# Rebuilding the front of an attention-then-MoE kernel: load order, masking and upsampling by matmul, and a first stage begun operand by operand

## The chip, the cores and the metric

The kernel runs on one core of a Trainium2 chip. The metric is device time in microseconds (us); a profile's span is a little shorter.

In the profile, PE is TensorE (matmul), PEld its weight loads, ACT ScalarE, DVE VectorE, POOL GpSimd, and SP SyncE, which issues DMAs. A trailing q (SPq, ACTq) is an engine's sequencer. "Half clock" means that the TensorE clock granted in the records was 0.50 instead of 1.00.

## The reference, cut to what matters

```python
# 8 batches, 8 heads, 576 tokens, head size 64
q_d, k_d, v_d = (mean over each 4 tokens of q, k, v)
out_up    = repeat(softmax(q_d k_d^T / 8) v_d, 4)                      # 144 tokens, upsampled
out_local = softmax(where(|i - j| < 4, q k^T / 8, -1e9)) v
x = (out_up + out_local) as [4608, 512]
h = x @ w_in                             # 512 -> 2048, "first stage"
out = (h * sigmoid(1.702 h)) @ w_out     # 2048 -> 512, "second stage"
```

## The kernel before

The MoE works on nine groups of 512 tokens. During group g, TensorE also does the attention of batch g+1, slipped in at fixed steps. So only the attention of batch 0 stands exposed, in the prologue. The first stage has 16 blocks of four matmuls (one per operand `xT[0..3]`, that is, per head pair), each block followed by a silu on ScalarE. The second stage has four output tiles of 16 matmuls.

The matmuls of this kernel write their results to PSUM. A tile of 512 FP32 columns is called one bank here, and the program declares eight of them: three two-bank tiles rotate in the attention, two one-bank accumulators rotate in the MoE:

```python
psA = tile_pool(name="psA", bufs=3, PSUM)       # [128, 2, 512] FP32: two banks each
psM = tile_pool(name="psM", bufs=2, PSUM)       # [128, 512] FP32: one bank each
...
def mm1(g, steps):
    for ffc in range(16):
        for f in steps.get(ffc, ()): f()        # attention of the next batch
        hps = psM.tile([128, TG], FP32, name="hps", tag="psM")
        for dmc in range(4):
            nc.tensor.matmul(hps, lhsT=w_in_bf[:, dmc, ...], rhs=xT[dmc][:, ...], ...)
        nc.scalar.activation(out=gT[:, ffc, :], in_=hps, func=AF.Silu, scale=1.702)
```

The prologue and the loads around it:

```python
load_v(0)                        # 10 DMAs issued by SyncE
load_qk(0, 0); load_qk(0, 1)     # issued by GpSimd (they cast to bf16)
...  # pooling on GpSimd, exp, band mask on VectorE, av, four normalisations, transposes
load_w_in(0, 512)                # issued on GpSimd after the pooling of batch 0
load_w_in(512, 512); load_w_in(1024, 1024)
for qd in range(2): load_qk(1, qd)
load_w_out(0)
...
for hp in range(4):              # transposes; upsampled part copied, then added ("merge")
    x[hp] = transp(y[hp]); merge(0, hp, x[hp], copy_od(x[hp]), ...)
load_v(1, gate=gate)             # SyncE
for c in range(1, 4): load_w_out(c)
...
osb = moe_sb.tile([128, n], FP32, name="osb", tag=f"osb{n}", bufs=3)   # scaled output, then a store on SyncE
```

The softmax here doesn't subtract the row's maximum and nothing guards it: scores larger than these inputs give would overflow.

## Time and profile before

| | |
|---|---|
| time | 337.35 us (337.05 to 337.67) |
| PE busy | 94% of the span |
| chain of waits | PE 84%, SPq 5%, DMA 4% |
| last operand of batch 0 ready | 31.47 us |
| TensorE idle in group 0 | 50.0 to 56.3 us |
| distance from one group's first silu to the next, from group 1 to group 7 | 33.5 to 34.4 us |

A row of the last kind says most about a steady state: it is read from the timeline as the start of the first silu of each group.

In the steady state (timeline of the kernel before, columns: start us, duration us, engine, line, operation, output<-inputs, shapes, count, idle time before and what ended it), a block of four matmuls passes every 0.86 us:

```profile
215.64 0.60 ACT L523 ACTIVATE gT<-hps 128x512 bf16<-128x512 f32 x1 [0.27 <-PE hps L517]
215.66 0.38 PE L517 MATMUL hps<-xT_83,w_in_bf 128*128 128x512 bf16 x1
215.88 0.38 PE L517 MATMUL hps<-xT_84,w_in_bf 128*128 128x512 bf16 x1
216.09 0.38 PE L517 MATMUL hps<-xT_85,w_in_bf 128*128 128x512 bf16 x1
216.31 0.38 PE L517 MATMUL hps<-xT_82,w_in_bf 128*128 128x512 bf16 x1
216.51 0.60 ACT L523 ACTIVATE gT<-hps 128x512 bf16<-128x512 f32 x1 [0.27 <-PE hps L517]
```

The matmuls start 0.216 us apart.

TensorE's longest waits (waits view; columns: total us, times, longest us):

```profile
PE vdp L272 <- POOL vb_87 L251: 6.3, 1, 6.3
PE sl_188 L299 <- DVE qT_179 L220: 3.3, 1, 3.3
```

The first is the hole in group 0: v of batch 1 is late. The windows view shows what it costs beyond the idle time (columns: window, its length, busy us of PE, PEld, DVE, ACT, POOL with counts, granted PE clock, DMA share, GB/s):

```profile
50.00:52.00 2.00, 0.01 (x1) 0.04 (x1) 0.00 (x0) 0.08 (x1) 0.00 (x0) 1.00 1.02 168
54.00:56.00 2.00, 0.00 (x0) 0.00 (x0) 0.00 (x0) 0.00 (x0) 2.00 (x1) 0.50 0.02 4
60.00:62.00 2.00, 2.00 (x6) 0.72 (x5) 0.56 (x2) 1.98 (x3) 0.00 (x0) 0.50 0.00 0
```

TensorE idles at 50 to 56, and afterwards works at half clock until about 62. The idle time began at 50.0, and the mean clock of 0.60 in the window from 52 to 54 puts the fall at about 52.4, so 2.4 us later. The clock came back at about 62.6 (mean 0.84 from 62 to 64), 6.3 us after the work had resumed.

### The profile page before, as it was taken

The page shows a single profiled execution, that of the slowest core. Times are in us where ns is not written, and L with a number is a line of the kernel's source. Part 1 is how long each engine was busy: PE and PEld are TensorE (multiplying, and loading weights), DVE is VectorE, ACT ScalarE, POOL GpSimd, SP SyncE. Part 2 cuts the span into 40 slices and gives each one's busy share as a digit, 9 for nine tenths or more (in the row PEclk, how much of TensorE's full clock was granted, in tenths as well). Part 3 has the DMA queues.
Part 4 walks back from the last instruction along what each step waited for, and adds up shares of the span by engine and source line. Part 5 has one row for each costly group of instructions (what it writes and reads, how often), then busy time and mean ns, then how long its engine had stood idle before and what let it go on. Part 6 is the DMA issues. An engine that isn't in the chain of part 4 may idle for free.

```text
span 336.2 us, 11213 instructions
## 1 busy us (share of the span) xinstructions
PE 315.9 (94%) x5013; PEld 157.4 (47%) x5013; DVE 135.3 (40%) x217; ACT 184.2 (55%) x315; POOL 138.6 (41%) x164
## 2 busy tenths in 40 slices
PE   6777993999999999999999999999999999999995
PEld 2343442454545455545554545455545554444444
DVE  5766710384067506750675066506750570000000
ACT  2346760546664667466746673668366737424611
POOL 6966802027940892089208920793079000000000
PEclk9699996799999999999999999999999999999999
DMA  8899992199991897199519951898180010011012
GB/s 148 150 159 211 196 200 42 67 181 198 262 190 68 164 204 139 64 181 204 120 67 188 204 114 66 161 208 135 66 163 13 33 67 31 2 63 62 0 55 71
DMA packets 63552, 41.36 MB, mean 123 GB/s; under 512 B 44048, under 2 KB 54416, under 8 KB 63504
## 3 DMA queue, kind: packets, MB, share of 16 engines
q1 hardware_dynamic: 55056, 26.95, 37.5%
q0 software_dynamic: 8304, 13.63, 23.0%
q8 instruction: 39, 0.64, 0.8%
q14 instruction: 9, 0.07, 0.1%
q10 hardware_dynamic: 144, 0.07, 0.1%
HBM read 44.83 MB, written 9.44 MB: 161 GB/s over the span
## 4 chain that ended last, share of the span: by engine, by line
PE 84%; SPq 5%; DMA 4%; POOL 2%; DVE 2%; issue 1%; ACT 1%; POOLq 0%; ACTq 0%
PE ops L558 36%; PE hps L517 33%; SPq L174 5%; DMA qb_128<-in_q_dram 2%; PE sd L315 2%; PE av L354 2%; PE xt L403 2%; PE av L376 2%; DMA vf<-in_v_dram 1%; PE ops L572 1%; PE vdp L272 1%; POOL vb_87 L251 1%; PE warm L465 1%; DVE y L389 1%; PE xt L413 0%
## 5 line engine op out<-in xcount | busy, mean ns | idle before, releaser
L558 PE MATMUL ops<-w_out_bf,gT 128*128 128x512 bf16 x560 | 129.8, 383 | 0.0
L523 ACT ACTIVATE gT<-hps 128x512 bf16<-128x512 f32 x144 | 86.0, 597 | 49.0 <-PE hps L517 49.0
L517 PEld LDWEIGHTS <-w_in_bf 128*128 128x128 bf16 x576 | 55.8, 98 | 68.4 <-issue 2.0
L558 PEld LDWEIGHTS <-gT 128*128 128x128 bf16 x560 | 52.2, 98 | 60.8 <-issue 2.1
L517 PE MATMUL hps<-xT_85,w_in_bf 128*128 128x512 bf16 x144 | 54.6, 379 | 0.8 <-DVE vf L590 0.8
L517 PE MATMUL hps<-xT_82,w_in_bf 128*128 128x512 bf16 x144 | 54.6, 379 | 0.0
L517 PE MATMUL hps<-xT_84,w_in_bf 128*128 128x512 bf16 x144 | 54.6, 379 | 0.0
L517 PE MATMUL hps<-xT_83,w_in_bf 128*128 128x512 bf16 x144 | 54.6, 379 | 0.0
L543 ACT ACTIVATE osb<-ops 128x512 f32<-128x512 f32 (+2 forms) x37 | 22.0, 595 | 40.4 <-PE ops L558 27.2
L340 DVE TENSOR_TENSOR es_90<-es_90,mask 128x600 bf16<-128x600 bf16 x8 | 7.6, 950 | 84.8 <-ACT es_90 L326 84.8
L425 ACT COPY od<-xt 128x384 f32<-128x384 f32 x64 | 21.1, 412 | 36.3 <-PE xt L413 30.8
L389 DVE TENSOR_TENSOR y<-av,rc 128x896 bf16<-128x896 f32 x32 | 34.9, 1092 | 1.1
L545 DVE TENSOR_SCALAR osb<-ops 128x128 f32<-128x128 f32 x1 | 0.3, 291 | 55.3 <-ACT osb L543 55.3
L387 DVE RECIPROCAL rc<-av 128x14 f32<-128x14 f32 x32 | 7.7, 240 | 19.6 <-PE av L376 19.6
L465 PE MATMUL warm<-wz 128*128 128x512 bf16 x41 | 14.1, 476 | 1.2 <-DVE wz L100 1.2
L251 POOL CAST vb_87<-vf 128x2560 bf16<-128x2560 f32 x4 | 9.4, 2344 | 13.1 <-DMA vf<-in_v_dram 13.1
L403 PEld LDWEIGHTS <-y 60*64 60x64 bf16 x640 | 7.4, 107 | 9.2 <-issue 4.3
L403 PE MATMUL xt<-ident,y 60*64 60x57 bf16 (+1 forms) x640 | 9.5, 194 | 1.3 <-issue 0.8
L340 DVE TENSOR_TENSOR es_92<-es_92,mask 128x600 bf16<-128x600 bf16 x8 | 4.2, 529 | 13.8 <-ACT es_92 L326 13.8
L482 ACT ACT_TABLE_LOAD x7 | 9.0, 1283 | 0.1
L478 ACT ACT_TABLE_LOAD x7 | 9.0, 1283 | 0.1
L446 DVE TENSOR_TENSOR xT_84<-xt,od 128x570 bf16<-128x570 f32 x8 | 6.0, 754 | 7.1 <-ACT od L425 7.1
(335 smaller groups left out, 382.5 us busy)
## 6 DMA issues: line engine op xcount, KB each, us to landing
vf<-in_v_dram SPq DMA_DIRECT2D x80, 128.0 KB, 6.6
out_dram<-osb SPq DMA_DIRECT2D x35, 256.0 KB, 2.1
v_96<-in_v_dram SPq DMA_DIRECT2D x36, 192.0 KB, 5.4
w_out_bf<-in_moe_w_out_dram POOLq DMA_DIRECT2D x4, 512.0 KB, 18.0
w_in_bf<-in_moe_w_in_dram POOLq DMA_DIRECT2D x2, 512.0 KB, 6.6
w_in_bf<-in_moe_w_in_dram POOLq DMA_DIRECT2D x1, 1024.0 KB, 11.6
kb_116<-in_k_dram POOLq DMA_DIRECT2D x1, 288.0 KB, 5.3
qb_118<-in_q_dram POOLq DMA_DIRECT2D x1, 288.0 KB, 6.7
```

Source lines behind the costliest of these rows:

```text
L174: nc.sync.dma_start(out=t[64 * par : 64 * par + 64, i], in_=bass.AP(tensor=v.tensor, offset=v[b, 0].offset + (114 * i + KSTART[par]) * D, ...
L251: cp(out=vbs[b % 2][:, i, h, 0:D], in_=vf[b][:, i, h])
L340: nc.vector.tensor_tensor(out=ev, in0=ev, in1=mask, op=ALU.mult)
L389: nc.vector.tensor_tensor(out=y, in0=ov[:, :, :, 0:D], in1=rc.to_broadcast([128, 2, 7, D]), op=ALU.mult,)
L403: nc.tensor.matmul(x[64 * j : 64 * j + 64, par, 57 * i + c0 : 57 * i + c1], lhsT=y[64 * pos : 64 * pos + 60, par, i, :], rhs=ident[64 * po ...
L425: nc.scalar.copy(out=od[:, 4 * t0 : 4 * (t0 + n)].rearrange("p (t f) -> p t f", f=4), in_=x[:, xx, 288 : 288 + n, None].to_broadcast([128, ...
L465: nc.tensor.matmul(t, lhsT=wz[:, 0:128], rhs=wz, start=True, stop=True)
L478: nc.scalar.preload_act_table_set("exp_and_others")
L517: nc.tensor.matmul(hps, lhsT=w_in_bf[:, dmc, ffc * 128 : (ffc + 1) * 128], rhs=xT[dmc][:, tok0 : tok0 + TG], start=(dmc == 0), stop=(dmc = ...
L523: nc.scalar.activation(out=gT[:, ffc, :], in_=hps, func=AF.Silu, scale=GELU_SCALE)
L543: eng.activation(out=osb, in_=ap, func=AF.Copy, scale=1.0 / GELU_SCALE)
L558: nc.tensor.matmul(ops[t], lhsT=gT[:, ffc, t * 128 : (t + 1) * 128], rhs=w_out_bf[:, ffc, :], start=(ffc == 0), stop=(ffc == n_ffc - 1),)
```

## The change

Its intent is to shorten the two stretches at the front that TensorE does not bound. The prologue is rebuilt: v of batch 0 waits for the first k and goes out on two queues (SyncE and ScalarE), w_in is gated behind a piece of v, the band mask of batch 0 is added in PSUM by matmul, and the upsampling becomes part of the transposing matmuls. Four PSUM tiles of two banks are held by name (`PA`), so that the four head pairs have one each. The first six blocks of group 0 are begun as each operand arrives. v of batch 1 now comes ahead of w_out 2 and 3, and the second stage of group 0 is reordered to need them late. The core of the diff, with cuts:

```diff
-    psA = ... tile_pool(name="psA", bufs=3, PSUM)
-    psM = ... tile_pool(name="psM", bufs=2, PSUM)
+    psum = ... tile_pool(name="psum", bufs=1, PSUM)
+    PA = [psum.tile([128, 2, 512], FP32, name=f"pa{i}") for i in range(4)]
+    PM = [PA[3][:, u, :] for u in range(2)]
+    def pm_tile():
+        turn["m"] += 1
+        return PM[turn["m"] % 2]
 ...
-            hps = psM.tile([128, TG], FP32, name="hps", tag="psM")
+            hps = acc[ffc % 8] if g == 0 else pm_tile()
 ...
-                ops[t] = psM.tile([128, d_model], FP32, name="ops", tag="psM")
+                ops[t] = PA[0][:, t - 2, :] if g == 0 and t > 1 else pm_tile()
 ...
+    load_v(0, gate=after_k, queues=(nc.sync, nc.scalar))
 ...
+    sp = scores(0, 0, barred=True)              # mask added in PSUM
+    nc.gpsimd.tensor_copy(out=w_in_bf[0:1, 0, 0:1], in_=vf[0][0:1, 1, 0, 0:1])
     load_w_in(0, 512)
 ...
+    warm(7); sd = scores_d(0, 0); ...; warm(4); ...; warm(5)    # dummy matmuls
+    prep_vd_pe(0, PA[3])
 ...
+    def spark(n):                               # short dummy matmuls
+        for _ in range(n):
+            nc.tensor.matmul(PA[3][:, 1, 456:512], lhsT=wz[:, 0:128], rhs=wz[:, 0:56], ...)
+    acc = [PA[n][:, u, :] for n in range(4) for u in range(2)]
+    spark(8); turned(0); spark(4); turned(1)    # turned: transp_sum and copy of one head pair
+    part((0, 1), 0); turned(2); ...; turned(3); part((0, 1, 2, 3), 2); ...
+    for ffc in range(6): silu(gT0, ffc, acc[ffc])
 ...
     def loads_2():
-        load_qk(2, 0, gate=gate); load_qk(2, 1)
-        load_v(2)
+        load_v(2, gate=gate)
         load_v4(2)
 ...
+            load_v(1, gate=after(w_out_bf[0:1, 0, 0:1], nc.vector))
+            nc.gpsimd.tensor_copy(out=w_out_bf[0:1, 8, 0:1], in_=vf[1][0:1, 2, 0, 0:1])
+            load_w_out(2); load_w_out(3)
```

More of the change, by code (lines that the diff above doesn't have):

```diff
@@ L51 @@
     moe_sb = ctx.enter_context(tc.tile_pool(name="moe_sb", bufs=1))
-    psA = ctx.enter_context(
-        tc.tile_pool(name="psA", bufs=3, space=bass.MemoryType.PSUM)
-    )
-    psM = ctx.enter_context(
-        tc.tile_pool(name="psM", bufs=2, space=bass.MemoryType.PSUM)
+    psum = ctx.enter_context(
+        tc.tile_pool(name="psum", bufs=1, space=bass.MemoryType.PSUM)
     )
@@ L69, with ps_tile @@
     kdT = [persist.tile([128, 160, 2], BF16, name=f"kdT{i}") for i in range(NQ)]
+    PA = [psum.tile([128, 2, 512], FP32, name=f"pa{i}") for i in range(4)]
+    PM = [PA[3][:, u, :] for u in range(2)]
+    turn = {"a": 0, "m": 0}
+    def ps_tile(n=None):
+        if n is None:
+            n = turn["a"] % 3
+            turn["a"] += 1
+        return PA[n]
+    def pm_tile():
+        turn["m"] += 1
+        return PM[turn["m"] % 2]
+    UP = 5 + 240
     wz = consts.tile([128, 512], BF16, name="wz")
+    off = consts.tile([128, 60], BF16, name="off")
     psel = consts.tile([128, 7, 64], BF16, name="psel")
+    up = consts.tile([128, UP, 4], BF16, name="up")
     PSEL = [(4, 2), (2, 1), (0, 0), (1, 0), (1, 1), (3, 1), (3, 2)]
@@ L78 @@
     dr = consts.tile([128, 1], FP32, name="dr")
+    du = consts.tile([128, UP], FP32, name="du")
+    ub = consts.tile([128, UP], BF16, name="ub")
+    rm = consts.tile([128, 1], FP32, name="rm")
     dp = consts.tile([128, 7, 64], FP32, name="dp")
@@ L97, in iota_mask, with iota_up @@
                            channel_multiplier=1, **it)
+    def iota_up():
+        for par in range(2):
+            nc.gpsimd.iota(du[halves[par]], pattern=[[1, UP]], base=-5 - 96 * par,
+                           channel_multiplier=-1, **it)
     def fill():
@@ L115, in make_mask @@
         nc.vector.tensor_single_scalar(out=dm, in_=dm, scalar=9.5, op=ALU.is_lt)
+        nc.vector.tensor_scalar(
+            out=off, in0=dm, scalar1=-1.0, scalar2=1e6, op0=ALU.add, op1=ALU.mult
+        )
         nc.scalar.copy(
@@ L122, in make_ident, with make_up, spread_up, make_psel @@
         nc.vector.tensor_single_scalar(out=ident, in_=di, scalar=0.0, op=ALU.is_equal)
-    def make_psel(dp, dr):
-        rv = consts.tile([128, 2], FP32, name="rv")
-        r2 = consts.tile([128, 2], FP32, name="r2")
+    def make_up():
+        nc.vector.reduce_sum(out=rm, in_=ident[:, 0:48], axis=mybir.AxisListType.X)
+        nc.vector.scalar_tensor_tensor(
+            out=du, in0=du, scalar=-192.0, in1=du, op0=ALU.add, op1=ALU.mult
+        )
+        nc.vector.tensor_scalar(
+            out=ub, in0=du, scalar1=0.0, scalar2=rm, op0=ALU.is_equal, op1=ALU.mult
+        )
+    def spread_up():
+        nc.scalar.copy(out=up, in_=ub[:, :, None].to_broadcast([128, UP, 4]))
+    rv = consts.tile([128, 2], FP32, name="rv")
+    r2 = consts.tile([128, 2], FP32, name="r2")
+    def make_psel():
         nc.vector.tensor_single_scalar(
@@ L141, in make_psel, with end_psel @@
         )
+    def end_psel():
         for sl, c in ((slice(0, 1), 1), (slice(1, 7), 0)):
@@ L165, in load_qk, with load_v @@
             store[b, qd] = t
-    def load_v(b, gate=None):
+    def load_v(b, gate=None, queues=(nc.sync, nc.sync)):
         t = ldp.tile([128, 5, H, D], FP32, name="vf", tag="vf")
@@ L171, in load_v @@
             gate(t[0:1, 0, 0, 0:1])
+            if queues[1] is not queues[0]:
+                gate(t[64:65, 0, 0, 0:1])
         for i in range(5):
             for par in range(2):
-                nc.sync.dma_start(
+                queues[par].dma_start(
                     out=t[64 * par : 64 * par + 64, i],
@@ L228, in prep_qk, with pool_q_reduce @@
         prep_1("q", b, qd)
+    def pool_q_reduce(b, qd):
+        t = work.tile([128, SD, 2], BF16, name=f"qdT{qd}", tag=f"qdT{qd}", bufs=1)
+        qdT[b, qd] = t
+        with nc.allow_low_precision("the sum is rounded once, as the pairwise one is"):
+            nc.vector.tensor_reduce(
+                out=t, in_=qT[b, qd].rearrange("p (j f) a -> p j a f", f=4),
+                axis=mybir.AxisListType.X, op=ALU.add,
+            )
     def pool_qk(b, qd, names="kq"):
@@ L284, in prep_vd_pe, with bar_others, scores @@
         )
-    def ps_tile(name):
-        return psA.tile([128, 2, 512], FP32, name=name, tag="psA")
-    def scores(b, qd):
-        sp = [ps_tile("sl0"), ps_tile("sl1")]
+    def bar_others(sp):
+        for par in range(2):
+            rows = slice(64 * par, 64 * par + 64)
+            for r in range(4):
+                nc.tensor.matmul(
+                    sp[r // 2][rows, r % 2, 0:300],
+                    lhsT=ident[rows, :],
+                    rhs=off[rows, None, :].to_broadcast([64, 5, 60]),
+                    start=True, stop=True,
+                    tile_position=(64 * par, 64 * par),
+                    skip_group_check=True,
+                )
+    def scores(b, qd, barred=False):
+        sp = [ps_tile(), ps_tile()]
+        if barred:
+            bar_others(sp)
         for i in range(5):
@@ L302, in scores, with scores_d @@
                             rhs=qT[b, qd][rows, q0 : q0 + 60, a],
-                            start=(a == 0), stop=(a == 1),
+                            start=(a == 0 and not barred),
+                            stop=(a == 1 or barred),
                             tile_position=(32 * r, 64 * par),
+                            skip_group_check=barred,
                         )
         return sp
-    def scores_d(b, qd, sd=None):
-        sd = sd or ps_tile("sd")
+    def scores_d(b, qd):
+        sd = ps_tile()
         for kc in range(3):
@@ L340, in mask_local, with av @@
             nc.vector.tensor_tensor(out=ev, in0=ev, in1=mask, op=ALU.mult)
-    def av(b, hp):
-        o = ps_tile("av")
+    def av(b, hp, n=None):
+        o = ps_tile(n)
         av_local(b, hp, o)
@@ L393, in normalise, with transp @@
         return y
-    def transp(y):
-        x = ps_tile("xt")
+    def transp(y, n=None):
+        x = ps_tile(n)
         for i in range(5):
@@ L420, in transp, with transp_sum, copy_x @@
         return x
+    def transp_sum(y, n):
+        x = ps_tile(n)
+        c0 = 20
+        for par in range(2):
+            edge = (0, 0) if par == 0 else (573, 285)
+            for i0, ni, slot, t0 in ((0, 5, 5, 0), (2 - par, 2, 6, -192)):
+                for j in range(2):
+                    base = c0 + 384 * j + t0
+                    nc.tensor.matmul(
+                        sub(x[64 * j : 64 * j + 64], 512 * par + 57 * i0 + 3 * (1 - par),
+                            (57, ni), (1, 57)),
+                        lhsT=y[:, j, slot, :],
+                        rhs=sub(up, base + 3 + 57 * par + 114 * i0, (114, ni), (1, 57)),
+                        start=(slot == 5), stop=True,
+                        tile_position=(0, 64 * j),
+                        skip_group_check=True,
+                    )
+            for j in range(2):
+                nc.tensor.matmul(
+                    x[64 * j : 64 * j + 64, par, edge[1] : edge[1] + 3],
+                    lhsT=y[:, j, 5, :],
+                    rhs=sub(up, c0 + 384 * j + edge[0], (1, 3)),
+                    start=False, stop=True,
+                    tile_position=(0, 64 * j),
+                    skip_group_check=True,
+                )
+        for i in range(5):
+            for par in range(2):
+                for j in range(2):
+                    pos = j if par == 0 else 1 - j
+                    c0 = 0 if (par == 1 or i == 0) else 3
+                    c1 = 60 if (par == 0 or i == 4) else 57
+                    nc.tensor.matmul(
+                        x[64 * j : 64 * j + 64, par, 57 * i + c0 : 57 * i + c1],
+                        lhsT=y[64 * pos : 64 * pos + 60, par, i, :],
+                        rhs=ident[64 * pos : 64 * pos + 60, c0:c1],
+                        start=False, stop=True,
+                        tile_position=(64 * pos, 64 * j),
+                        skip_group_check=True,
+                    )
+        return x
+    def copy_x(b, hp, x):
+        t0 = b * S
+        nc.scalar.copy(
+            out=sub(xT[hp], t0 + 3, (57, 2), (114, 5), (1, 57)),
+            in_=sub(x, 3, (509, 2), (57, 5), (1, 57)),
+        )
+        nc.scalar.copy(
+            out=sub(xT[hp], t0, (573, 2), (1, 3)),
+            in_=sub(x, 0, (512 + 285, 2), (1, 3)),
+        )
     def copy_od(x):
@@ L462, in warm @@
         if n:
-            t = psM.tile([128, 512], FP32, name="warm", tag="psM")
+            t = pm_tile()
             for _ in range(n):
@@ L467, in warm, with attention @@
                 )
-    def attention(b):
+    def attention(b, slots=None):
         st = {}
@@ L490, in f @@
             def f():
-                for hp in hps:
-                    st["o", hp] = av(b, hp)
+                for n, hp in enumerate(hps):
+                    st["o", hp] = av(b, hp, slots and slots[n])
                 for hp in hps:
@@ L498, in f @@
             def f():
-                for hp in hps:
-                    st["x", hp] = transp(st["y", hp])
+                for n, hp in enumerate(hps):
+                    st["x", hp] = transp(st["y", hp], slots and slots[n])
                 for hp in hps:
@@ L506, in attention, with hps_mm, new_gT, silu @@
         return [lambda: s_pe(0), lambda: s_act(0), s1, avn(0, 1), avn(2, 3), tr(0, 1), tr(2, 3)]
-    def mm1(g, steps):
-        tok0 = g * TG
-        gT = moe_sb.tile([128, n_ffc, TG], BF16, name="gT", tag="gT")
-        for ffc in range(n_ffc):
+    def hps_mm(g, ffc, dmc, acc):
+        nc.tensor.matmul(
+            acc,
+            lhsT=w_in_bf[:, dmc, ffc * 128 : (ffc + 1) * 128],
+            rhs=xT[dmc][:, g * TG : g * TG + TG],
+            start=(dmc == 0), stop=(dmc == n_dmc - 1),
+        )
+    def new_gT():
+        return moe_sb.tile([128, n_ffc, TG], BF16, name="gT", tag="gT")
+    def silu(gT, ffc, acc):
+        nc.scalar.activation(
+            out=gT[:, ffc, :], in_=acc, func=AF.Silu, scale=GELU_SCALE
+        )
+    def mm1(g, gT, steps, first=0):
+        for ffc in range(first, n_ffc):
             for f in steps.get(ffc, ()):
                 f()
-            hps = psM.tile([128, TG], FP32, name="hps", tag="psM")
+            hps = acc[ffc % 8] if g == 0 else pm_tile()
             for dmc in range(n_dmc):
-                nc.tensor.matmul(
-                    hps,
-                    lhsT=w_in_bf[:, dmc, ffc * 128 : (ffc + 1) * 128],
-                    rhs=xT[dmc][:, tok0 : tok0 + TG],
-                    start=(dmc == 0), stop=(dmc == n_dmc - 1),
-                )
-            nc.scalar.activation(
-                out=gT[:, ffc, :], in_=hps, func=AF.Silu, scale=GELU_SCALE
-            )
-        return gT
+                hps_mm(g, ffc, dmc, hps)
+            silu(gT, ffc, hps)
     def mm2(g, gT, steps):
@@ L532, in mm2 @@
         if g == 0:
-            order = [(t0 + u, c * 4 + f) for t0 in (0, 2) for c in range(4)
+            order = [(t0 + u, 4 * c + f)
+                     for t0, c in ((0, 0), (0, 1), (2, 0), (2, 1),
+                                   (0, 2), (2, 2), (0, 3), (2, 3))
                      for u in range(2) for f in range(4)]
@@ L569, in mm2 @@
                 cols = slice(256 * h, 256 * h + 256)
-                p = psM.tile([128, d_model], FP32, name="ops", tag="psM")
+                p = pm_tile()
                 for ffc in range(n_ffc):
@@ L586, with after, after_k @@
     POS = [13, 16, 33, 42, 53, 62, 71]
-    POS_0 = [14, 16, 34, 48, 56, 64, 72]
+    POS_0 = [16, 18, 27, 54, 68, 60, 76]
+    VDP_0 = 52
     gate = lambda t: nc.vector.memset(t, 0.0)
     o, y, x = {}, {}, {}
-    load_v(0)
+    def after(src, eng):
+        return lambda t: eng.tensor_copy(out=t, in_=src)
+    nc.scalar.preload_act_table_set("exp_and_others")
     load_qk(0, 0)
-    nc.scalar.preload_act_table_set("exp_and_others")
+    iota_mask()
     iota_psel()
     load_qk(0, 1)
-    iota_mask()
+    iota_up()
     fill()
-    warm(17)
-    make_psel(dp, dr)
+    warm(22)
     make_mask()
+    make_ident(di)
+    make_psel()
+    k_halves = iter((kf[0, 0][0:1, 0:1], kf[0, 0][64:65, 0:1]))
+    def after_k(t):
+        nc.vector.tensor_copy(out=t, in_=next(k_halves))
+    load_v(0, gate=after_k, queues=(nc.sync, nc.scalar))
     prep_1("k", 0, 0)
@@ L605 @@
     pool_qk(0, 0)
-    sp = scores(0, 0)
+    sp = scores(0, 0, barred=True)
     exp_local(0, sp)
     prep_qk(0, 1)
-    pool_qk(0, 1)
+    nc.gpsimd.tensor_copy(out=w_in_bf[0:1, 0, 0:1], in_=vf[0][0:1, 1, 0, 0:1])
     load_w_in(0, 512)
-    warm(3)
-    sd = scores_d(0, 0)
-    exp_down(0, sd)
-    mask_local(0)
-    warm(2)
-    sp = scores(0, 1)
-    exp_local(1, sp)
-    mask_local(1)
-    make_ident(di)
-    warm(5)
-    sd = scores_d(0, 1)
-    exp_down(1, sd)
-    prep_v(0, nc.scalar, i=slice(0, 2), h=slice(0, 4))
-    prep_v(0, nc.vector, i=slice(2, 5), h=slice(0, 4))
-    prep_v(0, nc.gpsimd, h=slice(4, 8))
+    pool_qk(0, 1, "k")
     load_w_in(512, 512)
@@ L630, with part, turned @@
     load_w_out(0)
-    warm(2)
-    for hp in range(2):
-        o[hp] = ps_tile("av")
-        av_local(0, hp, o[hp])
-    prep_vd_pe(0, ps_tile("vdp"))
-    nc.scalar.preload_act_table_set("silu_and_others")
-    warm(2)
-    for hp in range(4):
-        if hp < 2:
-            av_down(0, hp, o[hp])
-        else:
-            o[hp] = av(0, hp)
-        y[hp] = normalise(o[hp])
-    warm(2)
-    for hp in range(4):
-        x[hp] = transp(y[hp])
-        merge(0, hp, x[hp], copy_od(x[hp]), eng=nc.gpsimd if hp < 2 else None)
-        warm(2)
-    load_v(1, gate=gate)
-    for c in range(1, 4):
-        load_w_out(c)
+    load_w_out(1)
+    make_up()
+    pool_q_reduce(0, 1)
+    end_psel()
+    spread_up()
+    warm(7)
+    sd = scores_d(0, 0)
+    exp_down(0, sd)
+    sp = scores(0, 1, barred=True)
+    exp_local(1, sp)
+    warm(4)
+    sd = scores_d(0, 1)
+    exp_down(1, sd)
+    nc.scalar.preload_act_table_set("silu_and_others")
+    for i in range(5):
+        prep_v(0, nc.vector, i=slice(i, i + 1))
+    warm(5)
+    prep_vd_pe(0, PA[3])
+    for hp in range(4):
+        o[hp] = PA[hp]
+        av_local(0, hp, o[hp])
+        if hp == 0:
+            av_down(0, 0, o[0])
+            y[0] = normalise(o[0])
+    for hp in range(1, 4):
+        av_down(0, hp, o[hp])
+        y[hp] = normalise(o[hp])
+    def spark(n):
+        for _ in range(n):
+            nc.tensor.matmul(
+                PA[3][:, 1, 456:512], lhsT=wz[:, 0:128], rhs=wz[:, 0:56],
+                start=True, stop=True,
+            )
+    gT0 = new_gT()
+    acc = [PA[n][:, u, :] for n in range(4) for u in range(2)]
+    def part(ffcs, *dmcs):
+        for dmc in dmcs:
+            for ffc in ffcs:
+                hps_mm(0, ffc, dmc, acc[ffc])
+    def turned(hp):
+        copy_x(0, hp, transp_sum(y[hp], hp))
+    spark(8)
+    turned(0)
+    spark(4)
+    turned(1)
+    part((0, 1), 0)
+    turned(2)
+    part((0, 1), 1)
+    part((2, 3), 0, 1)
+    turned(3)
+    part((0, 1, 2, 3), 2)
+    part((4, 5), 0, 1, 2)
+    part(range(6), 3)
+    for ffc in range(6):
+        silu(gT0, ffc, acc[ffc])
     def loads_2():
-        load_qk(2, 0, gate=gate)
-        load_qk(2, 1)
-        load_v(2)
+        load_v(2, gate=gate)
         load_v4(2)
@@ L661 @@
         if g == 0:
-            prep_1("k", 1, 0)
-            prep_1("q", 1, 0)
+            nc.vector.memset(v4[32:64], 0.0)
+            prep_qk(1, 0)
             pool_qk(1, 0)
             prep_qk(1, 1)
+            load_v(1, gate=after(w_out_bf[0:1, 0, 0:1], nc.vector))
             pool_qk(1, 1)
-            nc.vector.memset(v4[32:64], 0.0)
-            prep_v(1, nc.gpsimd)
+            nc.gpsimd.tensor_copy(
+                out=w_out_bf[0:1, 8, 0:1], in_=vf[1][0:1, 2, 0, 0:1]
+            )
+            load_w_out(2)
+            load_w_out(3)
+            for i in range(5):
+                prep_v(1, nc.gpsimd, i=slice(i, i + 1))
+            for qd in range(NQ):
+                load_qk(2, qd)
         elif b < B:
@@ L684 @@
         if b < B:
-            for n, f in zip(POS if g else POS_0, attention(b)):
+            for n, f in zip(POS if g else POS_0, attention(b, None if g else (1, 2))):
                 steps.setdefault(n, []).append(f)
             if g == 0:
-                steps[POS_0[2]].insert(0, lambda: prep_vd_pe(1, ps_tile("vdp")))
-                steps[POS_0[3]].append(loads_2)
-        gT = mm1(g, steps)
+                steps.setdefault(VDP_0, []).append(lambda: prep_vd_pe(1, PA[2]))
+                steps[POS_0[5]].append(loads_2)
+        gT = new_gT() if g else gT0
+        mm1(g, gT, steps, 0 if g else 6)
         mm2(g, gT, {n - 16: f for n, f in steps.items() if n >= 16})
```

## The prediction

> **What bounds it now.** From group 1 on, TensorE: the two MoE lines dominate the chain of waits, and in the timeline full-width matmuls start every 0.216 us without a gap. Two stretches at the front are not bound by it.
> (a) Prologue. In the timeline the fourth MoE matmul, which needs the last operand of batch 0, starts at 31.52 us; three are done before it, so the dense stream effectively starts at about 30.9. The chain there: q landing at 12.6, pooling, masks, the v casts (until 19.5), v down-sampling, four normalisations of about 1.3 us on VectorE (22.3 to 27.4), merges until 31.4.
> (b) A hole in group 0. TensorE idles from 50.0 to 56.3 (waits: 6.3 us for the batch-1 v cast, itself waiting for DMA). v of batch 1 is issued last, beside three w_out loads, and lands at 53.7. The slice view then shows the granted clock at 0.5 until about 62. [...] Between 50.0 and 64.3 stand 14 matmuls, the down-sampling and one score block: about 5.4 us at full clock (estimate from the same blocks elsewhere in the trace). They take 14.3, so the hole costs 8.9.
>
> **What the change does.**
> - v of batch 0 follows k instead of sharing the DMA with it; w_in is requested at about 11 instead of 16.2, so the DMA lull at 14 to 18 us (0.46 and 0.18 busy) goes.
> - Masking moves into PSUM (16 more short matmuls); four VectorE masks of 0.7 to 2.1 us go. One pooling moves to VectorE (about 1.3). Normalisation starts at about 20.5.
> - Upsampling joins the transposing matmuls: od copies and merges (0.70 and 0.66 on ScalarE, 1.4 on GpSimd) become one ScalarE copy of about 0.9 per head pair; only the last stays exposed.
> - 18 first-stage matmuls (3.9 us) are done before the last operand exists (at about 27).
> Effective start about 23.2: 7.7 us saved, all on the critical path.
> - v of batch 1 goes ahead of w_out 2 and 3; the reordered second stage needs v only at its matmul 36. About 9.2 MB must land, at about 192 GB/s as before: v at about 47.5, the last w_out at about 51, against needs at about 47.7 and 52. So the hole shrinks to 0 to 3 us, without a clock drop. I expect 1.5 us lost here, and 0.7 in group 1, where GpSimd finished the batch-2 v sums only 0.5 us before use (96.15 against 96.67) and is now later relative to it.
> Groups 2 to 8 are unchanged.
>
> **Sum.** 337.35 - 7.7 - 8.9 + 1.5 + 0.7 gives 323; a somewhat earlier prologue is as likely as not. I predict 322.0 us, range 317.5 to 327.5. Chances: faster by over 2% 0.95, within 2% 0.04, slower 0.01.
>
> **What would show it.** First MoE matmuls of group 0 at 22 to 25 with no half clock under them; fourth-operand matmuls at 26 to 28; no TensorE wait above 3 us for the batch-1 v cast, granted clock 1.0 from about 20 on; DMA busy without a lull from 8 to 50; no TensorE wait over 1.5 us in group 1; groups 2 to 8 as long as before.
>
> **What would make it wrong.** Three queues sharing the DMA could delay the second k and q, which now head the VectorE order before all v casts (prologue saves under 4 us). [...] If DMA keeps ahead, there are no stalls and the time is 318.

337.35 - 7.7 - 8.9 + 1.5 + 0.7 is 322.95. The 8.9 are the 14.3 us of the trace less the estimate of 5.4 at full clock. That a hole of up to 3 us comes "without a clock drop" was not shown when it was written (e8 later had a wait of 3.0 us at a clock of 1.00). The 9.2 MB agree with the sizes of the loads on the page before (k, q and v of two batches, w_in, w_out: 8960 KB), and the 192 GB/s lie within its windows from 36 to 46 us (188 to 196). The pooling of about 1.3 and the copy of about 0.9 are estimates; the changed kernel shows 1.34 (L275) and 0.64 + 0.17 (L530, L534).

## The result, and the profile after

The changed kernel takes 487.97 us (486.66 to 491.96, 5 runs) against 337.67 for the kernel before beside it. The ratio is 1.447, with an interval of 1.441 to 1.453. Ratios here are the mean time of one kernel's fast runs over that of the other's fast runs of the same rounds, so they are not quite the ratio of the medians quoted. The output is correct.

TensorE's waits after (same columns as before):

```profile
PE pa L626 <- ACT gT L637: 96.6, 119, 14.5
PE pa L682 <- ACT osb L667: 19.4, 23, 1.2
PE pa L682 <- ACT gT L637: 5.5, 8, 0.7
PE pa L626 <- ACT osb L667: 4.8, 7, 0.7
PE pa L782 <- DVE y L453: 4.3, 1, 4.3
```

L626 is the first-stage matmul, L682 the second-stage one, L782 the short dummy matmul. The first four lines sum to 126.3 us of MoE matmuls waiting for ScalarE, of which 14.5 are the hole described below. Before there was no such line. The reader should note the counts: 119 waits among 144 blocks. Most of the loss is not in the rebuilt front but spread over all nine groups. The steady state shows it (timeline after):

```profile
201.49 0.60 ACT L637 ACTIVATE gT<-pa 128x512 bf16<-128x512 f32 x1 [1.11 <-PE pa L626]
202.14 1.02 PE L626 MATMUL pa<-xT,w_in_bf 128*128 128x512 bf16 x4 [0.68 <-ACT gT L637]
203.20 0.60 ACT L637 ACTIVATE gT<-pa 128x512 bf16<-128x512 f32 x1 [1.11 <-PE pa L626]
203.85 1.02 PE L626 MATMUL pa<-xT,w_in_bf 128*128 128x512 bf16 x4 [0.69 <-ACT gT L637]
```

A block now takes 1.71 us: four matmuls, then the silu, then the next four matmuls. The silu of 201.49 ends at 202.09, and the next block starts at 202.14. That next block writes the *other* half of the tile and yet waits for the silu of this one. The distance from group to group rose from 33.5 to 49.9 us.

Three further faults are visible at the front. The last operand of batch 0 is ready at 39.38 us instead of 31.47. The dummy matmuls wait 4.3 us (the last line above). And there is a new hole at the start of group 1, 14.5 us of idle TensorE, of which this is the cause (timeline after):

```profile
75.58 6.74 SPq L215 DMA_DIRECT2D vf<-in_v_dram  x9
82.36 3.05 SPq L227 DMA_DIRECT2D v<-in_v_dram  x6
85.52 9.70 SPq L672 DMA_DIRECT2D out_dram<-osb  x4
94.26 0.60 ACT L667 ACTIVATE osb<-pa 128x512 f32<-128x512 f32 x1 [15.09 <-DMA out_dram<-osb]
```

The four stores of group 0 stand behind sixteen loads in SyncE's order (ten of vf and six of v; the view begins after the first). The fourth scaled tile needs the buffer of the first store, because there are three buffers. Its scaling starts only at 94.26, and the silu that TensorE needs comes after it on ScalarE, at 94.75.

What the change aimed at in group 0 did come: no wait for v of batch 1 is listed.

### The profile page after: what moved, and what is told of

Its sections match the earlier page's. It is cut to its first block, busy times and chain, and to the rows that moved or that the text cites. A ratio compares the mean times of both kernels' runs of the same rounds, so it can differ in the third digit from the quotient of the medians.

```text
span 490.2 us, 11291 instructions
## 1 busy us (share of the span) xinstructions
PE 346.5 (71%) x5062; PEld 158.7 (32%) x5062; DVE 127.2 (26%) x219; ACT 183.8 (37%) x313; POOL 133.3 (27%) x165
## 4 chain that ended last, share of the span: by engine, by line
PE 61%; ACT 25%; issue 6%; DMA 4%; SPq 2%; DVE 2%; ACTq 0%; DVEq 0%; POOLq 0%
PE pa L626 30%; PE pa L682 21%; ACT gT L637 16%; ACT osb L667 4%; PE pa L361 2%; DMA out_dram<-osb 2%; ACT L599 2%; DMA vf<-in_v_dram 1%; SPq L215 1%; PE pa L379 1%; ACT ed L396 1%; PE pa L467 1%; DVE y L453 1%; DMA kb<-in_k_dram 1%; ACT od L542 1%
## 5 line engine op out<-in xcount | busy, mean ns | idle before, releaser
L626 PE MATMUL pa<-xT,w_in_bf 128*128 128x512 bf16 x576 | 150.5, 386 | 101.9 <-ACT gT L637 96.6
L682 PE MATMUL pa<-w_out_bf,gT 128*128 128x512 bf16 x560 | 132.4, 379 | 25.8 <-ACT osb L667 19.4
L637 ACT ACTIVATE gT<-pa 128x512 bf16<-128x512 f32 x144 | 85.3, 598 | 155.4 <-PE pa L626 155.4
L626 PEld LDWEIGHTS <-w_in_bf 128*128 128x128 bf16 x576 | 55.5, 98 | 192.7 <-issue 142.4
L682 PEld LDWEIGHTS <-gT 128*128 128x128 bf16 x560 | 51.6, 97 | 85.4 <-issue 29.1
L404 DVE TENSOR_TENSOR es<-es,mask 128x600 bf16<-128x600 bf16 x28 | 13.2, 472 | 212.5 <-ACT es L390 211.2
L667 ACT ACTIVATE osb<-pa 128x512 f32<-128x512 f32 (+2 forms) x37 | 21.8, 590 | 64.4 <-PE pa L682 36.0
L453 DVE TENSOR_TENSOR y<-pa,rc 128x896 bf16<-128x896 f32 x32 | 34.9, 1092 | 1.1
L390 ACT ACTIVATE es<-pa 128x600 bf16<-128x600 f32 x32 | 19.7, 668 | 18.7 <-PE pa L361 9.7
L563 DVE TENSOR_TENSOR xT<-pa,od 128x570 bf16<-128x570 f32 x28 | 21.1, 753 | 18.7 <-ACT od L542 18.6
L307 POOL TENSOR_TENSOR v<-v 112x512 f32<-112x512 f32 x18 | 22.7, 1263 | 0.0
L261 DVE STREAM_TRANSPOSE kT<-kb 128x576 f32<-128x576 f32 x16 | 20.0, 1248 | 0.7 <-DMA kb<-in_k_dram 0.6
L261 DVE STREAM_TRANSPOSE qT<-qb 128x576 f32<-128x576 f32 x16 | 19.8, 1237 | 0.6 <-DMA qb<-in_q_dram 0.6
```

Of the source, the lines that this page charges most:

```text
L261: nc.vector.transpose(out=t32.rearrange("p (i c) -> p c i", c=18), in_=store[b, qd].bitcast(FP32).rearrange("p (c d) -> p c d", c=18),)
L307: eng.tensor_tensor(out=t1[0:112], in0=x[:, :, 0:2, :], in1=x[:, :, 2:4, :], op=ALU.add)
L390: nc.scalar.activation(out=es[2 * qd + u][:, :, 0:300], in_=sp[u][:, :, 0:300], func=AF.Exp, scale=inv_sqrt_d,)
L453: nc.vector.tensor_tensor(out=y, in0=ov[:, :, :, 0:D], in1=rc.to_broadcast([128, 2, 7, D]), op=ALU.mult,)
L563: eng.tensor_tensor(out=sub(xT[hp], t0 + 3, (57, 2), (114, 5), (1, 57)), in0=sub(x, 3, (509, 2), (57, 5), (1, 57)), in1=sub(od, 3, (57, 2) ...
L626: nc.tensor.matmul(acc, lhsT=w_in_bf[:, dmc, ffc * 128 : (ffc + 1) * 128], rhs=xT[dmc][:, g * TG : g * TG + TG], start=(dmc == 0), stop=(d ...
```

## The experiments

Theory A: the framework keeps its automatic waits per tile, not per slice or bank, so two accumulators that are slices of one tile act as a single buffer. Rival B: something on the chip or on ScalarE made the blocks slower. Twelve kernels were run (no e11). Each round also ran the kernel before on the same chip (medians 336.8 to 337.4).

### e1: two tiles instead of two slices

```diff
-    PA = [psum.tile([128, 2, 512], FP32, name=f"pa{i}") for i in range(4)]
+    PA = [psum.tile([128, 2, 512], FP32, name=f"pa{i}") for i in range(3)]
+    PA.append(psF.tile([128, 2, 512], FP32, name="pa3"))       # psF: closed after the prologue
 ...
+    front.close()                                              # then, on the same two banks:
+    PM[:] = [psM.tile([128, 512], FP32, name=f"pm{u}") for u in range(2)]
+    acc[6:8] = PM
```

> The changed kernel with one thing altered: after the prologue the two accumulators of the MoE stages are two separate one-bank tiles on the same two banks, instead of two slices of one two-bank tile. Theory A (waits are kept per tile, so the two slices act as one buffer and TensorE waits for each silu): TensorE's waits for ScalarE fall from about 126 us to under 20, a stage of four matmuls takes 0.86 us again instead of 1.71, and the time is 345 to 365 us. Rival B (the waits come from the chip or from ScalarE being slower, not from how the buffers are declared): time stays near 488. The late prologue and the hole at the start of group 1 should remain under either.

It took 353.54 us (ratio 1.045, 1.039 to 1.051): 134 us of the loss went. The timeline of e1 shows the silus 0.86 us apart again and TensorE without a break:

```profile
230.72 5.56 PE L629 MATMUL pm<-xT,w_in_bf 128*128 128x512 bf16 x24
231.78 0.60 ACT L640 ACTIVATE gT<-pm 128x512 bf16<-128x512 f32 x1 [0.27 <-PE pm L629]
232.65 0.60 ACT L640 ACTIVATE gT<-pm 128x512 bf16<-128x512 f32 x1 [0.27 <-PE pm L629]
```

By the program the banks are the same, the traces of both kernels hold 5062 weight loads, and the output is correct: only the declaration differs. The wait was bookkeeping and protected nothing here: e1 does without it on the same two banks, at 0.86 us a block instead of 1.71.

### e2: the kernel before with slices

```diff
-    psM = tile_pool(name="psM", bufs=2, PSUM)
+    PM = psM.tile([128, 2, 512], FP32, name="pm")              # bufs=1
+    def pm_tile(): turn[0] += 1; return PM[:, turn[0] % 2, :]
-        hps = psM.tile([128, TG], FP32, name="hps", tag="psM")
+        hps = pm_tile()                                        # likewise ops, warm
```

> The kernel before with one thing altered: its two one-bank accumulators become two slices of one two-bank tile, everything else as it was. Theory A: every first-stage block of four matmuls again takes 1.71 us instead of 0.86 (0.85 times 16 times 9 is 122) and each output block costs about 0.7 more (25 in all), less what the hole in group 0 hides: 465 to 490 us. Rival B: 337 to 340 us.

It took 477.57 us (ratio 1.418). Group distances are 50.1 to 50.6 us up to group 7, and the waits are those of the changed kernel:

```profile
PE pm L524 <- ACT gT L530: 87.7, 128, 0.7
PE pm L565 <- ACT osb L550: 21.4, 25, 1.2
```

This one declaration, put into the kernel before, does nearly all the damage (140 us). Rival B falls.

### e3: dummy matmuls aimed elsewhere

```diff
-    def spark(n):   ... PA[3][:, 1, 456:512]
+    def spark(n, hp): ... PA[hp][:, 1, 456:512]                # spark(8, 0); spark(4, 1)
```

> As e1, and the dummy matmuls [...] write into the tile of the head pair that is transposed next, not into the one that the fourth normalisation still reads. Theory A predicts the same per-tile wait at this place: TensorE's 4.3 us wait for the fourth normalisation goes, the first transposes start about 4 us earlier and overlap the normalisations, the half clock under the first MoE matmuls goes too; 4 to 7 us faster than e1. Rival: VectorE's four normalisations end the chain anyway (30.4 us), gain under 2 us.

It took 352.25 us (1.045): no gain over e1, a miss. The wait for the fourth normalisation did go, but a pause stood at almost the same place, "PE pa L785 <- issue: 2.7, 1, 2.7". "issue" means that the engine waited for nothing that the profile shows. (The removed wait does not tell tile from slice: the dummy columns 456 to 511 lie in the slice of 512 columns of which the normalisation reads columns 0 to 454.)

### e4: ScalarE issues four v loads instead of five

```diff
-                queues[par].dma_start(
+                queues[par if i < 4 else 0].dma_start(
```

> As e3, and the last of the five v loads that ScalarE issues is issued by SyncE instead, so ScalarE no longer waits for an earlier load to land before its first exp. Theory: the first exp moves from 13.2 to about 10, the second scores from 14.0 to about 12.2, and the v down-sampling from 22.7 to 19 to 20; 2 to 4 us faster than e3. Rival (v landing at 18.6 is the bound): under 1 us.

It took 351.99 us (1.043), within noise of e3: also a miss. The first exp did move as expected, from 13.05 in e3 to 10.29. But the second scores then ran into another pause of the same kind, "PE pa L364 <- issue: 3.6, 1, 3.6" (1.0 in e3), and the v down-sampling came at 21.46 instead of 21.92. Splitting v over two issuing engines held ScalarE in the changed kernel from 5.96 to 13.18, during which it could not start an exp. No run of the changed kernel issues v from one engine alone, so what the split gains was not measured. What the trace shows is a price.

### e5: a fourth output buffer

```diff
-            osb = moe_sb.tile([128, n], FP32, name="osb", tag=f"osb{n}", bufs=3)
+            osb = moe_sb.tile([128, n], FP32, name="osb", tag=f"osb{n}", bufs=4)
```

> As e4, with four buffers instead of three for the scaled output tiles. Theory: the hole at the start of group 1 (TensorE waits 10.2 us for the first silu, then runs at half clock to about 93) comes from ScalarE waiting for a free output buffer, because the four stores of group 0 all stand behind sixteen v loads in SyncE's order; with a fourth buffer ScalarE doesn't wait. The wait goes, and with it the half clock: 10 to 15 us faster than e4, 335 to 341 us. Rival (the hole is late k, q or v of batch 2): no change.

It took 340.25 us (1.009), 11.7 less than e4. The stores still stand behind the loads, but ScalarE passes (timeline of e5):

```profile
78.68 3.05 SPq L230 DMA_DIRECT2D v<-in_v_dram  x6
81.83 2.43 SPq L675 DMA_DIRECT2D out_dram<-osb  x4
75.50 0.60 ACT L670 ACTIVATE osb<-pa 128x512 f32<-128x512 f32 x1
77.08 0.60 ACT L640 ACTIVATE gT<-pm 128x512 bf16<-128x512 f32 x1 [0.99 <-PE pm L629]
```

### e6: no two neighbouring blocks of group 0 in one tile

```diff
-            hps = acc[ffc % 8] if g == 0 else pm_tile()
+            hps = acc[(0, 2, 4, 6, 7, 6, 7, 6)[ffc - 8] if ffc > 7 else ffc] if g == 0 else pm_tile()
```

> As e5, and from the ninth first-stage block of group 0 on no two blocks in a row use the two halves of one tile. Theory (waits per tile): the remaining three waits of TensorE for the silu of group 0 (2.5 us) go; 2 to 3 us faster than e5. Rival: nothing.

It took 337.88 us (ratio 1.000, 0.996 to 1.005), 2.4 less than e5. Of TensorE's waits in e5 this line is gone in e6:

```profile
PE pa L629 <- ACT gT L640: 2.5, 3, 1.1
```

Theory A holds at this third place too. With all this mended, the change only equals the kernel before, although it has no hole in group 0. The traces show where the gain went: the 24th first-stage weight load starts at 40.55 us in e6 and at 35.62 in the kernel before, 4.9 later. (Weight loads are counted because a few matmul records are missing in e6.) From there to the first silu of group 1 it takes 34.1 us instead of 39.9, so 5.8 less, and group 1 takes 1.2 more. The prologue lost most of what the missing hole gave.

### e7, e12 and e10: the pauses called "issue"

In the packets of the instruction queue, 16 KB each, a pattern stood out: TensorE paused after 446 or 447 and after 956 of its instructions (matmuls and weight loads, as the trace records them; a matmul or two may be missing), and each pause ended 1.3 to 1.7 us after such a packet had landed (twelve pauses in the changed kernel, e3 to e7 and e12). The queue moves 39 such packets (0.64 MB) in the changed kernel and in e6 and 40 in e7, which has 132 TensorE instructions more. Theory F: these are TensorE running out of instructions, because its fetch is held up by the loads that fill the DMA. e7 replaces the first 22 dummy matmuls of 512 columns by 88 of 128 columns:

```diff
-    warm(22)
+    t = pm_tile()
+    for _ in range(88):
+        nc.tensor.matmul(t[:, 0:128], lhsT=wz[:, 0:128], rhs=wz[:, 0:128], start=True, stop=True)
```

> As e6, with the first 22 dummy matmuls of 512 columns replaced by 88 of 128 columns: the same columns, 132 more TensorE instructions before the first scores. Theory F (the pauses of TensorE at about its 450th and 960th instruction, each ended 1.2 to 1.4 us after a 16 KB packet of the instruction queue landed, are TensorE running out of fetched instructions while the loads fill the DMA): the pause now falls about 130 instructions earlier in the program, before the first transpose, or there is one more; the first MoE matmul comes 1 to 5 us later. Rival (the pause belongs to those transposes and their data): same place in the program, same time within 1 us.

The pause moved as F says, and the time did not. In e6 it fell among the dummies before the second transpose, in e7 among the av matmuls, after 956 instructions in both (timelines of e6, then e7):

```profile
27.08 0.35 PE L521 MATMUL pa<-ident,y 60*64 60x60 bf16 x20
27.55 0.24 PE L785 MATMUL pa<-wz 128*128 128x56 bf16 x3
30.52 0.23 PE L785 MATMUL pa<-wz 128*128 128x56 bf16 x1 [2.73 <-issue]
```

```profile
21.92 0.52 PE L443 MATMUL pa<-vd,ed 48*64 48x65 bf16 x37
26.96 0.65 PE L443 MATMUL pa<-vd,ed 48*64 48x65 bf16 x23 [4.52 <-issue]
```

The time was 338.82 us (1.009, 1.003 to 1.015), and in the profiled run the last operand was ready at 36.5 against 38.5 in e6, not later (this run of e7 was its fastest, that of e6 its slowest). The expected delay is a miss: the first pause also came earlier in the program, and it was shorter, 1.7 us against 3.7. e12 tests the other half of F, that the loads cause it:

```diff
     y[3] = normalise(o[3])
+    nc.gpsimd.tensor_copy(out=w_in_bf[0:1, 0, 0:1], in_=y[3][0:1, 0, 0, 0:1])
+    load_w_in(0, 512); load_w_in(512, 512); load_w_in(1024, 1024)   # moved here from above
+    load_qk(1, 0); load_qk(1, 1); load_w_out(0); load_w_out(1)
```

> As e6, with every load of w_in, of k and q of batch 1 and of w_out 0 and 1 held back until the fourth normalisation has ended (about 29 us), so that the DMA is nearly idle from about 19 to 29 us. A diagnostic, not an improvement: group 0 then starts late. Theory F (the pauses are TensorE's instruction fetch held up by the loads that fill the DMA): the pause at about the 958th TensorE instruction, 2.7 us in e6, shrinks to under 1 us. Rival (the fetch takes that time whatever the loads do): it stays at 2.5 us or more.

The second pause is gone (timeline of e12), and the windows of e6 and e12 show what differs, the DMA share in the last but one column:

```profile
25.78 0.35 PE L521 MATMUL pa<-ident,y 60*64 60x60 bf16 x20
26.25 0.24 PE L786 MATMUL pa<-wz 128*128 128x56 bf16 x3
26.69 0.20 PE L786 MATMUL pa<-wz 128*128 128x56 bf16 x1 [0.20 <-issue]
```

```profile
26.00:28.00 2.00, 1.39 (x43) 1.15 (x42) 1.93 (x5) 0.51 (x1) 0.00 (x0) 1.00 1.12 211
30.00:32.00 2.00, 1.48 (x34) 1.19 (x35) 1.31 (x2) 0.00 (x0) 0.00 (x0) 0.50 1.11 210
```

```profile
26.00:28.00 2.00, 1.35 (x52) 1.01 (x40) 1.93 (x5) 1.07 (x3) 0.00 (x0) 1.00 0.04 8
```

In e12 the packet started at 24.31, when TensorE had begun 869 instructions and had some left. In e6 it started at 28.23, after 956, when TensorE had already stopped. The first pause (3.6 us, from 13.2 to 16.8) stayed in e12, as it should: k, q and v fill the DMA there in both (share 0.99 to 1.37 from 12 to 16 us in e12). The second window of e6 also shows the price that followed the pause: half clock, which lasted until 36.5, under the first MoE matmuls. (The total of e12, 341.96 us in one run, says nothing, since its group 0 starts late on purpose.)

By these runs the supply of instructions was not hidden in this prologue while the DMA was full: TensorE paused 2.7 us after the 956th TensorE instruction in e6 at a DMA share of 1.12, against 0.2 at 0.04 in e12.

e10 drops the 7, 4 and 5 dummy matmuls that stand in the exposed chain:

```diff
-    warm(7)
-    warm(4)
-    warm(5)
```

> As e6, without the three groups of 7, 4 and 5 dummy matmuls between the first scores and the v down-sampling. Theory: under the half clock that follows the first pause in TensorE's instruction supply they take 0.43 us each and stand in TensorE's order before the v down-sampling, which is then ready but waits (v casts done at 17.7, down-sampling at 22.3): it starts about 3 us earlier, the first silu too; 2 to 4 us faster than e6. Rival (they keep the clock up, as intended): slower or the same.

It took 334.69 us (0.993, 0.988 to 0.998). That is 3.2 less than e6 by the medians and 2.4 by the ratios, whose intervals overlap a little. The v down-sampling started at 18.24 instead of 22.20, though at half clock (timelines of e6, then e10):

```profile
22.20 1.28 PE L325 MATMUL pa<-vb,psel 128*64 128x256 bf16 x14
18.24 1.71 PE L325 MATMUL pa<-vb,psel 128*64 128x256 bf16 x14
```

In e6 the last v cast, which the down-sampling needs, ended at 18.0. Dummies that are meant to keep the clock up stood, after a pause of 3.7 us in which it had halved (0.51 from 16 to 18 us, 0.50 from 18 to 22, in e6), in TensorE's order ahead of work that was ready. Without them the clock stayed at 0.50 from 14 to 32 us in e10, where e6 had 1.00 from 24 to 28. The edit also shifts the pauses in TensorE's instructions, so how much of the gain is the dummies' alone was not separated.

### e8, e9 and e13: the load order in the kernel before

e8 takes one idea of the change alone:

```diff
     load_v(1, gate=gate)
-    for c in range(1, 4): load_w_out(c)
+    load_w_out(1)
 ...                                             # in group 0, after the pooling of batch 1:
+            nc.gpsimd.tensor_copy(out=w_out_bf[0:1, 8, 0:1], in_=vf[1][0:1, 2, 0, 0:1])
+            load_w_out(2); load_w_out(3)
```

> The kernel before with only the load order of the change: w_out 2 and 3 are issued once the third piece of v of batch 1 has landed, instead of beside it. Theory: v is in by about 46, before its use at the 18th second-stage matmul, and w_out 2 and 3 by 49 and 53, just before theirs; the 6.3 us wait and the half clock after it go: 327 to 331 us. Rival (the DMA's total rate is the bound, so w_out becomes the late one): 332 to 338 us.

It took 332.51 us (ratio 0.986, 0.983 to 0.989): its whole interval lies below 1, and it is the fastest kernel run here. Its first waits are:

```profile
PE ops L558 <- issue: 5.4, 34, 0.2
PE ops L558 <- DMA w_out_bf<-in_moe_w_out_dram: 3.0, 1, 3.0
PE sl L299 <- DVE qT L220: 2.8, 2, 2.0
PE av L376 <- POOL vd L260: 1.7, 1, 1.7
```

A wait of 6.3 us that halved the clock (0.50) became one of 3.0 that did not (1.00 from 50 to 56 us). The rival is partly right: w_out is now the late one. Two attempts to go further failed:

e9:

```diff
+    load_w_in(0, 512)
     pool_qk(0, 1)
-    load_w_in(0, 512)
 ...
-            osb = ... bufs=3)
+            osb = ... bufs=4)
 ...
-                steps[POS_0[3]].append(loads_2)
+                steps[POS_0[2]].append(loads_2)
```

> As e8, with three more moves meant to win time: the first w_in load is issued before the pooling of the second k and q (fills the DMA lull at 14 to 18 us, so all later loads come about 3 us earlier), the loads of batch 2 are issued at step 34 instead of 48, and four output buffers so that stores behind those loads block nobody. Theory: the 3.0 us wait for w_out and the 2.0 and 1.7 us waits in group 1 shrink to under 1 each: 326 to 330 us. Rival (the early w_in delays the first batch by as much): 331 to 334 us.

e13, against e8:

```diff
     load_w_out(1)
+    load_w_out(2)
 ...
-            nc.gpsimd.tensor_copy(out=w_out_bf[0:1, 8, 0:1], in_=vf[1][0:1, 2, 0, 0:1])
-            load_w_out(2); load_w_out(3)
+            nc.gpsimd.tensor_copy(out=w_out_bf[0:1, 12, 0:1], in_=vf[1][0:1, 2, 0, 0:1])
+            load_w_out(3)
 ...                                             # and the last two edits of e9
```

> An attempt at a version that beats both. As e8, but only w_out 3 is held back behind v of batch 1 (in e8 TensorE waited 3.0 us for w_out 2, which was issued only at 46); and from e9 the loads of batch 2 at step 34 and the fourth output buffer, but not the earlier w_in. Theory: w_out 2 and v both arrive before their uses at 49 and 51, w_out 3 at about 53 before its use, and group 1 loses its waits of 2.0 and 1.7 us as in e9: 326 to 330 us. Rival (DMA total rate: v is late instead by 1 to 3 us): 330 to 333 us.

e9 took 335.30 us (0.995), and its first silu came at 33.94 instead of 31.74 in e8. The early w_in is the likely cause: in e13, which leaves it out, the first silu came at 32.45. e13 took 335.68 us (0.994): v of batch 1 was late by 4.0 us instead, and the clock fell to a mean of 0.66 for 55 to 60 us. Group 1 did shorten in both, from 35.5 to 33.6 or 33.7, but the gain was lost in group 0. In both the rival named the right place, but its range of times was missed too.

## Why the prediction was wrong, point by point

- **"Groups 2 to 8 are unchanged."** This step failed, and it alone is about four fifths of the miss (134 of 166 us). The group distance rose from 33.5 to 49.9 us, and e1 and e2 show the cause: two slices of one tile in place of two tiles (134 us taken away by e1, 140 added by e2). The prediction does not mention the new PSUM declarations: I had read that part of the diff as the same eight banks under other names.
- **"I expect ... 0.7 in group 1."** It was 14.5 us of idle TensorE and half clock after it (0.50 from 94 to 102 us); e5 puts its cost at 11.7 us. I had looked at when batch 2 is needed, not at what else stands in SyncE's order. With second-stage tiles finishing together at the end, four stores meet three buffers behind sixteen loads.
- **"Effective start about 23.2: 7.7 us saved."** The last operand was to be ready at about 27 and was ready at 39.38. Even with the other faults mended (e6) it was 38.49, later than before. The terms that were mis-sized: normalisation began at 25.13, not 20.5 (before: 22.26); the early head pairs did not overlap the normalisations, first by the 4.3 us wait of the dummies, then, with that gone, by a pause of 2.7 in the instruction supply; and half clock (0.50 from 30 to 36 us in the changed kernel and in e6) lay under the first MoE matmuls. I had added up durations of engines and data and left out both TensorE's own instruction stream and the dummies in its order. In the kernel before, the pause among the transposes was only 0.8 us (at 27.4).
- **"So the hole shrinks to 0 to 3 us"** was right for the changed load order: no wait for v or w_out of group 0 is listed in e6, and e8 confirms the idea in the kernel before. No one length of idle time parts the cases, though: a wait of 3.0 us in e8 did not halve the clock (1.00 from 50 to 56 us), a pause of 2.7 us in e6 was followed by half clock (0.50 from 30 to 36), and a wait of 4.0 us in e13 by a mean of 0.66 from 55 to 60. The 8.9 us were sized high for what could be kept in the kernel before: e8 gained about 4.3, since w_out was then late by 3.0 and group 1 grew from 34.3 to 35.5.
- **"Three queues sharing the DMA could delay the second k and q"** was a fear that did not come true: the second q was transposed at 10.82, against 12.62 before.
- **The sum.** From 487.97: e1 takes 134.4, e3 and e4 together 1.6 (within noise), e5 11.7, e6 2.4 and e10 3.2. That leads to 334.7. The remaining 12.7 to my 322 I put down mainly to the prologue (in e10 the last operand comes at 36.1, against my 27). That is an account of the difference, not a run of its own. Whether the prologue could reach its planned time with a denser instruction stream was not tried.

## What to carry to other kernels

Double buffering lives in the declaration: two slices of one tile may share one set of waits (here 1.71 us a block instead of 0.86), so check after any change of buffers that the steady state still overlaps, before looking at what the change was for. When stores and later loads share an issuing engine, count how many output buffers must be free before the first store gets its turn (here a fourth buffer took 11.7 us off, e5). When an engine pauses with "issue" as the only reason, in a stretch of very many short instructions while the DMA is full, compare the place in its program with the packets of the instruction queue (here 2.7 us in e6, 0.2 in e12).
